# A recurrent attention kernel: one home for the x rows, the residual rows in the place of the attention weights, and an eighth of a streamed weight unit kept in SBUF

## The chip, the cores and the metric

The kernel runs on one core of a Trainium2 chip. The metric is the device time of one execution in microseconds (us); the figure for a kernel is the median of several runs. A profile is one execution recorded instruction by instruction. In it, PE is TensorE (matmuls), PEld its weight loads, DVE is VectorE, ACT is ScalarE, POOL is GpSimd and SP is SyncE, which here only issues DMAs.

## The reference

The output is the sum of three things over 2048 tokens of width 1024: the input, a dense part, and a recurrent attention part. Both parts work on the layer-normed input `xn`.

```python
def _A_ref(x, mem0, Wq, Wk, Wv, Wo, seg_len):      # seg_len 32, 32 heads of 128
    scale = Dh ** (-0.5)                           # M = 8 memory rows
    mask = (idx[:, None] < M) | (idx[:, None] >= idx[None, :])
    mem = mem0
    for s in range(n_seg):                         # 64 segments
        h = concatenate([mem, xs], axis=1)         # 8 + 32 rows
        q, k, v = h @ Wq, h @ Wk, h @ Wv
        p = softmax(where(mask, q @ k.T * scale, -1e9))
        o = (p @ v) @ Wo
        mem = o[:, :M, :]                          # the next segment's memory
        outs.append(o[:, M:, :])
    return concatenate(outs, axis=1)

def _B_ref(x, w1, b1, w2, b2):                     # 1024 -> 3584 -> 1024
    return gelu(x @ w1 + b1) @ w2 + b2

return x + _A_ref(xn, ...) + _B_ref(xn, ...)
```

A segment's memory is the attention output of the segment before it, so the 64 segments run one after the other.

## The kernel before

**Two phases.** The first phase computes the layer norm, the dense part and the input's own share of the sum, and writes the sum of these two to DRAM as *residual rows* (`res_d`, and `resL_d` for the left rows below). It also writes the normed input, transposed, as *x rows* (`rows_d`). In the second phase the 64 segments run in order. The index of a segment within a group of four is called `i4`.

**Left rows.** A segment has 32 x rows and 8 memory rows, 40 in all, while TensorE's column tiles here are 32 wide. So each segment's main pass carries 24 of the x rows and the 8 memory rows. The last 8 x rows of four segments are *left rows*, 32 together, and go through the same weights in passes of their own, spread over the segments of a group. Their output product runs in segments with `left_o` (`i4 == 1`, and the last one): 16 times, and once more at the end.

**The weights.** The four projections are 64 *units* of 128 x 2048 bf16 numbers (512 KB): the half passes K0, Q0, K1, Q1, V0 and V1 of eight units each, and O with sixteen. 47 units stay in SBUF. 17 do not fit and are *streamed*: 15 of them come from DRAM in every segment, and two are kept in four PSUM banks and copied by VectorE (`copy_bits`, line 273). There are six slots for streamed units. When a unit has been used (`unit_done`), SP issues the DMA of the next streamed unit into its slot (`start_stream`, line 284). So the order of the transfers is the order of the units, six ahead at most.

**One segment.** The x rows with the memory rows are TensorE's weights in the K, Q and V passes (line 830); they stand in one of two homes of 128 x 256, `homes[s % 2]`, the two halves of `hr_home`. While the passes run, scores, exponentials, sums and the weighted values of the two halves of heads are put between units at fixed positions (`SCORES_0`, `SUMS_0`, `VALUES_1` and so on). `sums` writes the attention weights to `pd_main` (line 1012), and `values` reads them (lines 1039 and 1045). The output pass O (`o_product`, line 1088) has 16 positions. In segments without left rows a position before the ninth takes two blocks of 256 columns per matmul, and later ones take one block; in segments with left rows all take two. Then `put_mem` turns the 8 memory rows and VectorE copies them into the next segment's x rows (line 330). The next K0 waits for this copy. After it, VectorE adds the residual rows (line 1246), and the sums are stored.

**Small DMAs of a segment.** They are issued by ACT in the first seven segments and by POOL after (`loads`). Ahead of the V passes the x rows of the next segment are loaded into the idle home (line 1155). After V1 the segment's own home is free, and the residual rows are loaded into it (line 1185); the sum is made in place, and four stores write it to the output from there (line 1279). In segments with left rows, the left residual rows are loaded to `pd_main` after position 6 of O (line 1211), the left sum is also made in place, and each of the two sums goes to a DRAM scratch `outL_d` in two stores of 64 partitions (line 1252). From there POOL copies the rows to the output, at the `unit_done` of the following segment (line 1276).

**Who shares which memory.** `v_home`, `outM` and the queries' home `q_home` are one stretch of the tile `kq`: `v_home` (512 columns) holds V and then, as `outM`, the second half of heads' values and the memory rows' source; `q_home` (640 columns) begins at the same column, and the next segment's queries are written to it (lines 909 and 925). `nat_home` is the first 512 columns of `d_oL`; it holds the first half of heads' values, which positions 0 to 7 of O read, and then the next segment's keys (line 882).

The order on each engine is the order in which the program is written (a manual schedule); waits between engines, and between a DMA and who reads or rewrites its memory, are put in by the framework as semaphores.

Of the kernel before, what the change touches and what calls it, by code (L numbers as in the profile page):

```python
# [10 lines left out]
BF16 = mybir.dt.bfloat16  # L11
# [3 lines left out]
ALU = mybir.AluOpType  # L15
PSUM = bass.MemoryType.PSUM

P = 128
S = 2048
DM = 1024  # L20
# [4 lines left out]
SEG = 32  # L25
MEM = 8
NSEG = S // SEG
KT = DM // P
# [9 lines left out]
NX = 24  # L38
NL = SEG - NX
GRP = 4  # L40
NGRP = NSEG // GRP
# [71 lines left out]
STREAMED_O = [unit for unit in ORDER[48:] if IS_STREAMED[unit]]  # L113

IN_BANKS = STREAMED_O[AT_BANKS]
KEPT = (IN_PSUM, IN_BANKS)
assert len(RESIDENT) == NUNIT - STREAMED


@with_exitstack  # L120
def kernel(
# [16 lines left out]
    nc = tc.nc  # L138
# [3 lines left out]
    out_flat = out.rearrange("b s d -> (b s) d")  # L142
# [6 lines left out]
    Wo_v = A_Wo.rearrange("h e d -> e h d")  # L149
# [8 lines left out]
    rowsL_d = dram.tile([NGRP + 1, P, 256], BF16, name="rowsL_d")  # L158
    resL_d = dram.tile([NGRP + 1, P, 256], BF16, name="resL_d")
    R_n = dram.tile([S, DM], BF16, name="R_n")  # L160
    outL_d = dram.tile([NGRP, 2 * SEG, DM], BF16, name="outL_d")


    place = nc.lookup_mloc("DynamicDMAScratchLoc")
# [15 lines left out]
    hrp = ctx.enter_context(tc.tile_pool(name="hrp", bufs=1))  # L180
    ctx.enter_context(tc.manual_schedule())

    homes = [hr_home[:, 0:256], hr_home[:, 256:512]]
    small_consts = consts.tile([P, 16], BF16, name="small_consts")
    bd, off = small_consts[:, 0:4], small_consts[:, 4:8].bitcast(F32)

# [3 lines left out]
        return slabs.tile([P, 2048], BF16, name="u", tag=place)  # L190


    ident = homes[1][:, 0:P]
    make_identity(nc, ident)
    ident_mem = nc.alloc_sbuf_tensor_at("ident_mem", [P, 4, NL], BF16, offset=SCRATCH + 3712)[:, :, :]
    nc.vector.tensor_copy(out=ident_mem[:, :, :], in_=ident.rearrange("p (j t) -> p j t", j=4)[:, :, NX:SEG])
# [78 lines left out]
    def start_stream(slot):  # L275
        if not starts:
            return
        n = starts.popleft()
        unit, t = streams[n], slab(slot)
        if unit in kept_in:  # L280
            for c0, bank in kept_in[unit]:
                copy_bits(t[:, c0:c0 + 1024].bitcast(U32), bank.bitcast(U32))
        elif unit in copies:
            nc.sync.dma_start(out=t[:, :], in_=copies[unit])
        else:
            fetch(t[:, :], unit)
        stream_tiles[n], slot_of[n] = t, slot
# [1 line left out]
    nxt, kept_in = {}, {}  # L289

    def load_x_rows(s, eng=nc.sync):
        eng.dma_start(out=homes[s % 2], in_=rows_d[s, :, :])
        nxt["hT"] = homes[s % 2].rearrange("p (k t) -> p k t", k=KT)

    def load_left_rows(g, eng=nc.sync):
        hr = hrp.tile([P, 256], BF16, name="hrL")
        eng.dma_start(out=hr[:, :], in_=rowsL_d[g, :, :])
        nxt["hL"] = hr.rearrange("p (k t) -> p k t", k=KT)
# [50 lines left out]
    with tc.tile_pool(name="ma", bufs=2) as ma:  # L349
# [235 lines left out]
        for tg in range(4):  # L585
            last = tg == 3
            if last:

                load_x_rows(0)
                load_left_rows(0)  # L590
                h = 4 * IN_BANKS[1] + 2 * IN_BANKS[2]
                nc.sync.dma_start(out=kq[:, 0:DM], in_=Wo_v[:, h, :])
                start_stream("xn0")
                start_stream("xn1")
                fetch_resident("late2", "xt0", "xt1")
# [140 lines left out]
    with tc.tile_pool(name="late", bufs=1) as late:  # L736
# [66 lines left out]
        for s in range(NSEG):  # L803
# [257 lines left out]
            def o_columns(t, k, blocks):  # L1061

                c0 = DM * k + 256 * blocks[0]
                if len(blocks) == 1:
                    return t[:, c0:c0 + 256]
                d = blocks[1] - blocks[0]
                return t[:, c0:c0 + 256 * (d + 1)].rearrange("p (n c) -> p n c", c=256)[:, ::d, :]

            def o_product(n, t, acc):


                unit = O_UNITS[n]
                w, i, u = unit
                for k in range(2):
                    h = 4 * (i % 4) + 2 * u + k
                    main = (outM if i >= 4 else nat_home)[:, h, :]
                    if left_o:
                        lhs = [(0, 32, left_outs[i // 4][:, h, :]), (32, 32, main)]
                        tiles = [(64 * r + r0, w, (2 * r, 2 * r + 1), lhsT) for r0, w, lhsT in lhs for r in range(2)]
                        start, stop = n == 0 and k == 0, n == 15 and k == 1  # L1080
                    elif n < NPAIR:
                        tiles = [(64 * k + 32 * r, 32, (r, r + 2), main) for r in range(2)]
                        start, stop = n == 0, n == NPAIR - 1
                    else:
                        tiles = [(32 * r, 32, (r,), main) for r in range(4)]
                        start, stop = n == NPAIR and k == 0, n == 15 and k == 1
                    for r0, rows, blocks, lhsT in tiles:
                        nc.tensor.matmul(  # L1088
                            acc[r0:r0 + rows, 0:256 * len(blocks)],
                            lhsT=lhsT,  # L1090
                            skip_group_check=True,
                            rhs=o_columns(t, k, blocks),
                            start=start,
                            stop=stop,
                            tile_position=(0, r0),
                        )
# [54 lines left out]
            turn_q(psQ1, (0, 10, 16))  # L1151
            if left_q[1] and not first:
                turn_qL(psQ1L, 1)
            if not final:
                load_x_rows(s + 1, loads)
            psV, psVL = half_pass("V", 0, left_v[0], {})
            if left_v[0]:
                left_values(0, psVL)
# [26 lines left out]
            loads.dma_start(out=homes[s % 2], in_=res_d[s + 1, :, :])  # L1185
            if first:
                load_left_rows(g + 1, loads)

# [8 lines left out]
            if apart:  # L1197
                at[VALUES_1[i4] + 1] = [moved_values]
            psX = new_acc()
            for n, unit in enumerate(O_UNITS):  # L1200
                t = unit_tile(unit)
                if n == NPAIR and not left_o:
                    st["folded"] = fold(psX)
                    psX = new_acc()
                o_product(n, t, psX)
                unit_done(unit)
                for fn in at.get(n, ()):
                    fn()
                if n == 6 and left_o:
                    st["resL"] = pd_main[:, 0:256]  # L1210
                    loads.dma_start(
                        out=st["resL"], in_=resL_d[og, :, :]
                    )
            nw = 2 if left_o else 1
            if not final:
                o_sb = outM
# [20 lines left out]
            res, rows = homes[s % 2], slice(s * SEG, s * SEG + NX)  # L1237
            tiles = (res, st["resL"]) if left_o else (res,)
            for w, r in reversed(list(enumerate(tiles))):
                if left_o:  # L1240
                    o = psX[:, 256 * w:256 * w + 256].rearrange("p (h e) -> p h e", e=32)
                else:
                    o = o_sb[:, 0:8, :]
                r_rows = r.rearrange("p (h e) -> p h e", e=32)
                to = d_oL[:, 256 * w:256 * w + 256].rearrange("p (h e) -> p h e", e=32) if final else r_rows
                nc.vector.tensor_tensor(out=to, in0=o, in1=r_rows, op=ALU.add)  # L1246
                if left_o and not final:

                    for b in range(2):
                        c0 = 256 * (2 * b + w)  # L1250
                        eng = nc.scalar if w else nc.gpsimd
                        eng.dma_start(out=outL_d[og, :, c0:c0 + 256], in_=r[64 * b:64 * b + 64, :])
# [5 lines left out]
            if final:  # L1258
                engines = [nc.sync, nc.scalar]
                n = 0  # L1260
                for b in range(2):
                    cs = slice(512 * b, 512 * b + 512)
                    pieces = [(rows, slice(64 * b + m0, 64 * b + m0 + NX))]
                    for sl, row in left_rows:
                        p0 = 64 * b + NL * sl
                        pieces.append((slice(row, row + NL), slice(p0, p0 + NL)))
                    for o, i in pieces:
                        engines[n % 2].dma_start(out=out_flat[o, cs], in_=d_oL[i, 0:512])
                        n += 1
            elif left_o:  # L1270
                pairs = [(out_flat[rows, :], outL_d[og, m0:m0 + NX, :])]
                pairs += [
                    (out_flat[row:row + NL, :], outL_d[og, NL * sl:NL * sl + NL, :]) for sl, row in left_rows
                ]
# [42 lines left out]
```

## Time and profile before

| | us |
|---|---|
| median of 3 runs | 1795.1 (1793.92 to 1796.6) |
| profiled execution, whole time | 1796.11 |
| its span, first to last instruction | 1794.4 |
| PE busy | 1696.3 (95%) |
| PEld busy | 889.3 (50%) |
| DVE busy | 983.8 (55%) |
| ACT busy | 683.6 (38%) |
| POOL busy | 300.4 (17%) |
| DMA moved | 594.44 MB, mean 331 GB/s |
| of it by SP's queue | 567.08 MB, 84.4% of the time of 16 DMA engines |
| granted TensorE clock | 1.000 |

The segments take the time from about 405 us on, some 21.5 us each. Of a row of the profile such as "L1012 DVE TENSOR_TENSOR pd_main<-kq,mixed 128x320 ... x128 | 62.5, 488 | 130.2 <-ACT mixed L999 130.2", L1012 is the line of the kernel, then come the engine, the operation, what is written from what, the shape, how often, the busy time in all, the mean of one in ns, and the idle time of the engine just before with what ended it. A row of waits reads: who waited, for whom, us in total, how often, the longest. A row of a timeline reads: start, duration, engine, line, operation, and in brackets the idle time before it and what ended it. ACTq and SPq are an engine's sequencer, which issues DMAs.

### The profile page before, as it was taken

How to read it: one execution, taken by the hardware profiler on the slowest of the kernel's cores; microseconds unless marked ns; L12 is line 12 of the kernel's file. 1: busy time of each engine (PE TensorE's matmuls, PEld its weight loads, DVE VectorE, ACT ScalarE, POOL GpSimd, SP SyncE). 2: the span in 40 equal slices, each digit the busy share in tenths (PEclk: the TensorE clock that was granted, in tenths of full speed). 3: DMA queues.
4: the chain of work that ended last, by engine and by line, in shares of the span. 5: the costliest groups of instructions: out<-in, count | busy, mean ns of one | idle time of the engine just before them, and what ended most of it. 6: DMA issues, size and time to landing. Idle time of an engine off the chain costs nothing.

```text
span 1794.4 us, 71508 instructions
## 1 busy us (share of the span) xinstructions
PE 1696.3 (95%) x31164; PEld 889.3 (50%) x31164; DVE 983.8 (55%) x2514; ACT 683.6 (38%) x1692; POOL 300.4 (17%) x586
## 2 busy tenths in 40 slices
PE   9999999999999999999999999999999989999988
PEld 5444444444555555545454555554545544554544
DVE  7656483825555555555455555555555554555544
ACT  6344251603333333334343434343434333433333
POOL 0000002301231111212122121121121111111111
PEclk9999999999999999999999999999999999999999
DMA  9455312789999999999999999999999999999998
GB/s 279 144 169 165 87 48 73 267 277 371 391 385 383 387 376 384 377 379 382 365 394 371 390 386 398 378 393 372 374 382 384 385 371 369 380 383 381 370 386 316
DMA packets 232830, 594.44 MB, mean 331 GB/s; under 512 B 57715, under 2 KB 88035, under 8 KB 232516
## 3 DMA queue, kind: packets, MB, share of 16 engines
q1 hardware_dynamic: 197584, 567.08, 84.4%
q0 software_dynamic: 16896, 16.85, 2.9%
q10 hardware_dynamic: 18036, 5.94, 1.3%
q8 instruction: 244, 4.00, 0.9%
q14 instruction: 70, 0.57, 0.1%
HBM read 573.43 MB, written 28.90 MB: 336 GB/s over the span
## 4 chain that ended last, share of the span: by engine, by line
PE 75%; DMA 11%; ACT 4%; DVE 4%; issue 4%; ACTq 1%; SPq 1%; POOL 0%; DVEq 0%; POOLq 0%
PE acc L830 38%; PE acc L1088 12%; PE ps L534 10%; DMA u<-Wc_O 8%; PE ps L662 6%; PE ps L693 3%; DMA u<-Wc_V 2%; ACT mixed L999 2%; PE acc L1039 1%; PE mixed L947 1%; DVE kq L914 1%; ACTq L459 1%; DVE pd_main L1012 1%; ACT kq L909 1%; SPq L521 1%
## 5 line engine op out<-in xcount | busy, mean ns | idle before, releaser
L830 PE MATMUL acc<-u,hr_home 128*32 128x512 bf16 x11520 | 758.8, 380 | 14.7 <-issue 8.3
L830 PEld LDWEIGHTS <-hr_home 128*32 128x32 bf16 x12288 | 350.3, 96 | 281.1 <-issue 33.2
L830 PE MATMUL acc<-u,hrL 128*32 128x512 bf16 x2880 | 256.2, 380 | 2.6 <-DVE qL L882 1.0
L534 PE MATMUL ps<-u 128*128 128x512 bf16 (+1 forms) x992 | 195.0, 358 | 0.0
L273 DVE TENSOR_SCALAR u<-kept 128x512 uint32<-128x512 uint32 x254 | 163.2, 684 | 56.9 <-PE acc L830 43.2
L1088 PE MATMUL acc<-u,d_oL 128*32 128x512 bf16 x2592 | 168.9, 380 | 13.1 <-issue 7.9
L882 ACT CAST d_oL<-acc 128x512 bf16<-128x512 f32 x143 | 82.0, 584 | 256.8 <-PE acc L830 251.5
L1088 PE MATMUL acc<-u,kq 128*32 128x256 bf16 (+1 forms) x2884 | 135.8, 310 | 13.6 <-DMA u<-Wc_O 11.2
L662 PE MATMUL ps<-u 128*128 128x512 bf16 x672 | 146.0, 379 | 0.0
L534 PEld LDWEIGHTS <-u 128*128 128x128 bf16 x992 | 91.6, 98 | 101.5
L1088 PEld LDWEIGHTS <-kq 128*32 128x32 bf16 x3908 | 103.0, 96 | 75.4 <-ACT kq L1058 21.2
L1012 DVE TENSOR_TENSOR pd_main<-kq,mixed 128x320 bf16<-128x320 bf16 x128 | 62.5, 488 | 130.2 <-ACT mixed L999 130.2
L914 DVE STREAM_TRANSPOSE kq<-kq 128x512 bf16<-128x512 bf16 x128 | 91.0, 711 | 73.2 <-ACT kq L909 71.0
L909 ACT CAST kq<-acc 128x512 bf16<-128x512 f32 (+2 forms) x192 | 85.4, 445 | 112.2 <-PE acc L830 82.6
L1279 POOL DMA_DIRECT2D out_dram<-hr_home x168 | 85.4, 516 | 221.7 <-DVE hr_home L1246 221.7
L886 ACT CAST kq<-acc 128x512 bf16<-128x512 f32 x128 | 75.2, 588 | 112.2 <-PE mixed L953 112.2
L830 PEld LDWEIGHTS <-hrL 128*32 128x32 bf16 x3072 | 87.9, 96 | 58.5 <-issue 7.6
L977 DVE TENSOR_TENSOR kq<-kq,mixed 128x96 bf16<-128x96 bf16 (+1 forms) x256 | 38.1, 190 | 125.8 <-ACT kq L967 72.6
L662 PEld LDWEIGHTS <-u 128*128 128x128 bf16 x672 | 65.5, 98 | 78.8 <-DVE u L619 0.4
L611 ACT ACTIVATE u<-ps,b1col 128x512 bf16<-128x512 f32 x112 | 76.5, 684 | 65.4 <-PE ps L534 62.3
L1088 PEld LDWEIGHTS <-d_oL 128*32 128x32 bf16 x2592 | 64.6, 96 | 67.7 <-issue 20.8
L999 ACT ACTIVATE mixed<-mixed,small_consts 128x160 f32<-128x160 f32 x256 | 94.2, 368 | 8.4
(126 smaller groups left out, 1911.2 us busy)
## 6 DMA issues: line engine op xcount, KB each, us to landing
u<-Wc_K SPq DMA_DIRECT2D x256, 512.0 KB
u<-Wc_V SPq DMA_DIRECT2D x256, 512.0 KB
u<-Wc_O SPq DMA_DIRECT2D x256, 512.0 KB
u<-Wc_Q SPq DMA_DIRECT2D x192, 512.0 KB
u<-in_B_w_dram SPq DMA_DIRECT2D x28, 512.0 KB
u<-in_A_Wq_dram SPq DMA_DIRECT2D x13, 512.0 KB
u<-in_A_Wv_dram SPq DMA_DIRECT2D x12, 512.0 KB
u<-in_A_Wk_dram SPq DMA_DIRECT2D x9, 512.0 KB
```

What stands on the lines that cost most here:

```text
L273: nc.vector.tensor_single_scalar(out=out, in_=in_, scalar=0, op=ALU.bitwise_or)
L534: nc.tensor.matmul(ps[:, SEG * s0:SEG * s1].rearrange("p (s t) -> p s t", t=SEG), lhsT=w1_sb[fb // 2][:, kt, (fb % 2) * P:(fb % 2 + 1) * P ...
L611: nc.scalar.activation(out=xb[:, :], in_=ps[:, :], func=ACT.Identity, bias=b1col[:, fb:fb + 1], scale=1.0)
L662: nc.tensor.matmul(ps[:, :], lhsT=gts[fc // 4][:, fc % 4, t * P:(t + 1) * P], rhs=w2_sb[fc // 2][:, fc % 2, cs], start=(fc == 0), stop=(fc ...
L830: nc.tensor.matmul(o, lhsT=lhs[:, i, :], rhs=m, start=(i == seq[0]), stop=(i == seq[-1]), tile_position=(0, 32 * j),)
L882: cp(out=out, in_=ps.rearrange("p (h e) -> p h e", e=32))
L909: nc.scalar.copy(out=q_home[:, h0:h1, NL:40], in_=ps[:, 32 * h0:32 * h1].rearrange("p (h e) -> p h e", e=32))
L914: nc.vector.transpose(out=home, in_=home)
L999: nc.scalar.activation(out=mixed[:, 160 * b:160 * b + 160], in_=mixed[:, 0:160], func=ACT.Exp, scale=-1.0, bias=off[:, b:b + 1],)
L1012: nc.vector.tensor_tensor(out=pdA.rearrange("p c b q -> p b c q"), in0=prA[:, None, :, :].to_broadcast([P, 2, 4, 40]), in1=dd, op=ALU.mult,)
L1088: nc.tensor.matmul(acc[r0:r0 + rows, 0:256 * len(blocks)], lhsT=lhsT, skip_group_check=True, rhs=o_columns(t, k, blocks), start=start, sto ...
L1279: loads.dma_start(out=out_flat[rows, 256 * j:256 * j + 256], in_=res[32 * j:32 * j + NX, :])
```

## The change

- `hr_home` now holds one home for the x rows; its other half, `part`, holds 256 of the 2048 columns of one streamed unit, `IN_PART` (the fourth streamed unit of O, at position 13). `part` is loaded once, in the dense phase. The unit's DMA in each segment is 1792 columns wide instead of 2048.
- Where a matmul of that unit took two blocks at once of which the last is kept, it is split into two of 256 columns each. That concerns segments with left rows: 68 more matmuls and weight loads in all.
- The x rows of the next segment are loaded after V1, into the one home, by ACT in all segments.
- The residual rows are loaded to `pd_main` after position 6 of O, the left residual rows to the first half of `nat_home` (`d_oL`) after position 8, both by ACT. The main sum is made in `pd_main` and stored from there. The left sum is made in `v_home` and stored from there.
- Each of the two sums of a segment with left rows goes to `outL_d` in one store of 128 partitions instead of two of 64; the layout of `outL_d` follows, and the copies from it to the output have two pieces per row.

```diff
-    homes = [hr_home[:, 0:256], hr_home[:, 256:512]]
+    home, part = hr_home[:, 0:256], hr_home[:, 256:512]
...
         elif unit in copies:
-            nc.sync.dma_start(out=t[:, :], in_=copies[unit])
+            c1 = 2048 - (256 if unit == IN_PART else 0)
+            nc.sync.dma_start(out=t[:, 0:c1], in_=copies[unit][:, 0:c1])
...
     def load_x_rows(s, eng=nc.sync):
-        eng.dma_start(out=homes[s % 2], in_=rows_d[s, :, :])
-        nxt["hT"] = homes[s % 2].rearrange("p (k t) -> p k t", k=KT)
+        eng.dma_start(out=home, in_=rows_d[s, :, :])
+        nxt["hT"] = home.rearrange("p (k t) -> p k t", k=KT)
...
+                w, i, u = IN_PART
+                nc.sync.dma_start(out=part, in_=Wo_v[:, 4 * i + 2 * u + 1, 768:1024])
...
+                if unit == IN_PART and k == 1 and blocks == (3,):
+                    return part
...
-                    for r0, rows, blocks, lhsT in tiles:
+                    if unit == IN_PART and k == 1:
+                        apart = [(r0, rows, (b,), lhsT, at) for at in range(len(tiles[0][2])) for r0, rows, blocks, lhsT in tiles for b in blocks[at:at + 1]]
+                    else:
+                        apart = [(*tile, 0) for tile in tiles]
+                    for r0, rows, blocks, lhsT, at in apart:
...
-            if not final:
-                load_x_rows(s + 1, loads)
             psV, psVL = half_pass("V", 0, left_v[0], {})
...
-            loads.dma_start(out=homes[s % 2], in_=res_d[s + 1, :, :])
+            if not final:
+                load_x_rows(s + 1, nc.scalar)
...
+            res, resL = pd_main[:, 0:256], d_oL[:, 0:256]
...
-                if n == 6 and left_o:
-                    st["resL"] = pd_main[:, 0:256]
-                    loads.dma_start(
-                        out=st["resL"], in_=resL_d[og, :, :]
-                    )
+                if n == 6:
+                    nc.scalar.dma_start(out=res, in_=res_d[s + 1, :, :])
+                if n == 8 and left_o:
+                    nc.scalar.dma_start(out=resL, in_=resL_d[og, :, :])
...
-                nc.vector.tensor_tensor(out=to, in0=o, in1=r_rows, op=ALU.add)
+                at = 256 * w
+                sums_at = d_oL[:, at:at + 256] if final else v_home[:, 0:256] if w else res
+                nc.vector.tensor_tensor(
+                    out=sums_at.rearrange("p (h e) -> p h e", e=32), in0=o, in1=r_rows, op=ALU.add
+                )
                 if left_o and not final:
-
-                    for b in range(2):
-                        c0 = 256 * (2 * b + w)
-                        eng = nc.scalar if w else nc.gpsimd
-                        eng.dma_start(out=outL_d[og, :, c0:c0 + 256], in_=r[64 * b:64 * b + 64, :])
+                    eng = nc.scalar if w else nc.gpsimd
+                    eng.dma_start(out=outL_d[og, :, 256 * w:256 * w + 256], in_=sums_at)
```

More of the change, by code (lines that the diff above doesn't have):

```diff
@@ L116 @@
 KEPT = (IN_PSUM, IN_BANKS)
+IN_PART = STREAMED_O[3]
 assert len(RESIDENT) == NUNIT - STREAMED
@@ L160 @@
     R_n = dram.tile([S, DM], BF16, name="R_n")
-    outL_d = dram.tile([NGRP, 2 * SEG, DM], BF16, name="outL_d")
+    outL_d = dram.tile([NGRP, P, 512], BF16, name="outL_d")
     place = nc.lookup_mloc("DynamicDMAScratchLoc")
@@ L190, in slab @@
         return slabs.tile([P, 2048], BF16, name="u", tag=place)
-    ident = homes[1][:, 0:P]
+    ident = part[:, 0:P]
     make_identity(nc, ident)
@@ L1059, in values, with o_columns @@
                     let_go(av[r])
-            def o_columns(t, k, blocks):
+            def o_columns(unit, t, k, blocks):
+                if unit == IN_PART and k == 1 and blocks == (3,):
+                    return part
                 c0 = DM * k + 256 * blocks[0]
@@ L1086, in o_product @@
                         start, stop = n == NPAIR and k == 0, n == 15 and k == 1
-                    for r0, rows, blocks, lhsT in tiles:
+                    if unit == IN_PART and k == 1:
[3 more added lines that the diff above has]
+                    for r0, rows, blocks, lhsT, at in apart:
                         nc.tensor.matmul(
-                            acc[r0:r0 + rows, 0:256 * len(blocks)],
+                            acc[r0:r0 + rows, 256 * at:256 * (at + len(blocks))],
                             lhsT=lhsT,
                             skip_group_check=True,
-                            rhs=o_columns(t, k, blocks),
+                            rhs=o_columns(unit, t, k, blocks),
                             start=start,
@@ L1236 @@
                     lead_products(LEAD)
-            res, rows = homes[s % 2], slice(s * SEG, s * SEG + NX)
-            tiles = (res, st["resL"]) if left_o else (res,)
+            rows = slice(s * SEG, s * SEG + NX)
+            tiles = (res, resL) if left_o else (res,)
             for w, r in reversed(list(enumerate(tiles))):
@@ L1244 @@
                 r_rows = r.rearrange("p (h e) -> p h e", e=32)
-                to = d_oL[:, 256 * w:256 * w + 256].rearrange("p (h e) -> p h e", e=32) if final else r_rows
-                nc.vector.tensor_tensor(out=to, in0=o, in1=r_rows, op=ALU.add)
+                at = 256 * w
[3 more added lines that the diff above has]
+                )
                 if left_o and not final:
-                    for b in range(2):
-                        c0 = 256 * (2 * b + w)
-                        eng = nc.scalar if w else nc.gpsimd
-                        eng.dma_start(out=outL_d[og, :, c0:c0 + 256], in_=r[64 * b:64 * b + 64, :])
+                    eng = nc.scalar if w else nc.gpsimd
+                    eng.dma_start(out=outL_d[og, :, 256 * w:256 * w + 256], in_=sums_at)
             let_go(psX)
@@ L1270 @@
             elif left_o:
[L1271 to L1274, printed above, removed]
+                made = outL_d[og, :, :].rearrange("(b r) c -> r b c", b=2)
+                pairs = [(out_flat[rows, :], made[m0:m0 + NX, :, :])]
+                pairs += [(out_flat[row:row + NL, :], made[NL * sl:NL * sl + NL, :, :]) for sl, row in left_rows]
+                pairs = [(o.rearrange("r (b c) -> r b c", b=2), r) for o, r in pairs]
                 for o, r in pairs:
```

## The prediction

> **What bounds the kernel now.** I read the page's slices first, then stretches of the span, then the waits, then the timeline at the places that the change touches.
>
> The page, time in 40 slices:
>
> ```profile
> PE   9999999999999999999999999999999989999988
> ...
> DMA  9455312789999999999999999999999999999998
> GB/s 279 144 169 165 87 48 73 267 277 371 391 385 383 387 376 384 377 379 382 365 394 371 390 386 398 378 393 372 374 382 384 385 371 369 380 383 381 370 386 316
> ```
>
> From slice 10 on (the 64 segments) both TensorE and the DMA engines are full. The stretches say how near to its limit each is. Segments 8 and 11 alone, then segments 8 to 59 together (us, busy time of the five engines, clock, DMA share, GB/s):
>
> ```profile
> 585.60:606.55 20.95, 20.21 (x470) 11.26 (x462) 11.77 (x32) 8.35 (x23) 3.74 (x7) 1.00 1.02 392
> ...
> 650.14:671.97 21.83, 20.34 (x470) 11.31 (x462) 11.26 (x30) 9.04 (x24) 3.78 (x7) 1.00 1.02 389
> 585.60:1705.90 1120.30, 1050.63 (x23694) 571.41 (x23686) 599.02 (x1549) 428.54 (x1170) 206.83 (x390) 1.00 1.00 380
> ```
>
> 1120.3 us for 52 segments is 86.2 us for a cycle of four (i4 = 0 to 3). The transfers could run at about 390 GB/s and run at 380: alone they would need 86.2 x 380/390 = 84.0. For TensorE I added up, from the starts of its streaming matmuls (lines 830 and 1088, normally 0.22 us per four), all that exceeds this spacing: 45.6 us in the 52 segments, 3.5 per cycle, nearly all at units that come from DRAM. So TensorE's own path is 86.2 - 3.5 = 82.7. The transfers bind by a little, and lateness of TensorE is partly free: 3.5 us per cycle is waiting for DMA anyway.
>
> The waits name those places, and a second kind, at the scores:
>
> ```profile
> PE acc L1088 <- DMA u<-Wc_O: 16.1, 27, 1.6
> PE mixed L947 <- DVE kq L914: 12.9, 40, 0.5
> ...
> PE acc L830 <- DMA u<-Wc_V: 5.4, 10, 1.3
> ```
>
> How long a small DMA takes beside this traffic stands at the lines of the residual load, the left residual load, the out stores, in this order (all POOL's, min/median/max), and in the chain:
>
> ```profile
> DMA to landing us min/median/max: 3.3/5.6/6.4
> ...
> DMA to landing us min/median/max: 2.9/4.7/5.5
> ...
> DMA to landing us min/median/max: 4.1/4.9/6.9
> ...
> 450.65 6.61 DMA pd_main<-resL_d
> ```
>
> The last was issued by ACT. ACT's other loads of the first seven segments show no landing, but VectorE waits for two: the residual issued at 493.19 released it at 499.63 (6.4 us), a left residual issued at 537.54 at 543.67 (6.1).
>
> **The change part by part**, in us after the last V1 matmul of a segment, the "own path" being segments without a DMA wait.
>
> *Bytes.* 64 KB of 15 streamed 512 KB units per segment stay in SBUF: 0.8% of 84.0 per cycle, -0.67. Against it, two loads per segment (x rows, residual) go from POOL to ACT. In the packet records POOL's 64 KB are 16 packets of 4096 bytes at 174 ns, ACT's 128 packets of 512 at 27.5 ns: 2.78 against 3.52 us of one engine, 0.046 of sixteen, twice per segment +0.37 per cycle. Transfers after: 83.7 (bounds 83.3, if small packets slip between large ones, to 84.0).
>
> *x rows.* Before, they were loaded into the idle one of two homes ahead of the V passes. Now the one home is V1's operand, so the load starts after V1 and is needed at the put of the memory rows (the copy on line 330), which waits for it, and the next segment's first matmul for that. The place in ACT's order is that of the old residual load, which ACT issued at 0.98 (i4 = 0 and 1), 0.67 (2) and 1.36 (3, where a second cast goes before it):
>
> ```profile
> 493.11 0.59 ACT L882 CAST kq<-acc 128x512 bf16<-128x512 f32 x1 [0.44 <-DVE kq L1017]
> 493.19 0.36 ACTq L1185 DMA_DIRECT2D hr_home<-res_d  x1
> ...
> 498.05 0.23 DVE L330 CAST hr_home<-mixed 128x64 bf16<-128x64 f32 x1 [0.57 <-PE mixed L320]
> ...
> 499.63 0.29 DVE L1246 TENSOR_TENSOR hr_home<-kq,hr_home 128x256 bf16<-128x256 bf16 x1 [1.36 <-DMA hr_home<-res_d]
> ```
>
> A load from here landed 1.4 us after the memory rows' copy; that was only VectorE's sum, now it is the copy itself. On the own path the copy starts at 5.8, 8.55, 6.2, 5.85 (i4 = 0 to 3). ACT's loads took 6.1 to 6.7, POOL's 4.7 when fewer streamed transfers were outstanding. TensorE will be later and fewer will be outstanding, so I take 5.5, between them: ready at 6.5, 6.5, 6.2, 6.9, late by 0.7, 0, 0, 1.05, in sum +1.7 per cycle. By 4.7: +0.2; by 6.7: 1.9 + 0 + 1.2 + 2.2 = +5.3.
>
> *Residual and out stores.* The residual (ACT, position 6 of O, issued near 2.4) lands at 7.9; VectorE's sum ends near 8.4 instead of 6.3 to 7.8. Next in VectorE's queue are the copies of the kept unit (1.3 us) and, 2.3 us after the copy of line 330, a transpose: covered. The four POOL stores now read pd_main and land 6.8 us after the sum (before: sum ended 6.7, last landed 13.4 for i4 = 0), at 15.2. The next weights are written to pd_main 9.0 to 9.2 after the copy of line 330, at 15.5 or later. Margin 0.3 to 0.8: I take 0; without it, up to 0.3 in three segments, +1.
>
> *Left sums (after i4 = 1).* The left residual goes to d_oL, which position 7 of O still reads: issue at 4.0, landed at 9.5 where the sum could start at 8.7. The sum goes to v_home, and ACT stores it from there 0.4 after the sum's start, at 9.9 (before, from pd_main, on average 9.8). The store lands 4.9 later, at 14.8. But v_home is where the next segment's queries are written: VectorE's left queries and ACT's cast both have to wait for this store, while before nothing wrote pd_main for 8.7 us. Segment 10's start shows when they come:
>
> ```profile
> 630.45 1.12 ACTq L1252 DMA_DIRECT2D outL_d<-pd_main  x2
> ...
> 633.41 0.18 DVE L925 COPY kq<-mixed 128x128 bf16<-128x128 bf16 x1
> 633.93 0.59 ACT L909 CAST kq<-acc 128x512 bf16<-128x512 f32 x1 [1.20 <-PE acc L830]
> 634.55 0.71 DVE L914 STREAM_TRANSPOSE kq<-kq 128x512 bf16<-128x512 bf16 x1 [0.96 <-ACT kq L909]
> 635.32 0.20 PE L947 MATMUL mixed<-kq,d_oL 128*32 128x40 bf16 x4
> ```
>
> Cast, transpose and scores follow without slack, 3.5 us after the store's issue. The own path has the cast at 12.6; 14.8 makes the scores, and all of TensorE behind them, 2.2 later. Bounds: loads of 4.7 and the quickest store (4.1) give +0.6, 6.7 and 5.8 give +4.3.
>
> *The rest.* 68 more matmuls of 256 columns take the place of halves of 512: the row has 273 against 380 ns, four side by side, 0.1 per cycle (0 to 0.2). ACT's issues cost 0.33 each, in gaps of 1 us and more: 0; without gaps 0.33 x 9. One store per left sum instead of two spares 0.5 of issue on ACT and POOL, already in the 4.9. The kept block costs one 64 KB load in the dense phase, 0.2.
>
> **Sum.** Own path 82.7 + 1.7 + 2.2 + 0.1 = 86.7; transfers 83.7. Now TensorE binds, by 3.0. Before, the cycle was 2.2 above the longer of the two, which stood 1.3 apart; at 3.0 apart I take 0.6 of DMA waits (0 to 2.2). Cycle 87.3, +1.1, times 63/4: +17 us. The profiled execution (1796.1, span 1794.4) is 1.0 above the median, 1795.1, so the prediction is 1812. 0.2% (3.6 us) is about what measuring this kernel can tell from no change.
>
> In the Trainium skill, "DMA: Bandwidth & Descriptors", section "Anatomy of one DMA — SWDGE (gpsimd) path", fits a DMA by 2.0 us + bytes/436e3: an estimate of 2.15 us for 64 KB. By it, no store or load here would be late and the sum would be the first rival's. The trace's 5.6 and 4.9 speak against it, in this traffic.
>
> **The rivals.** *1, faster: nothing lands late.* The left residuals landed in 4.7, the last ones, with hardly a stream outstanding, in 2.9. If TensorE's first lateness thins the queue so far that x rows land within 4.5 us of issue (5.85 - 1.36), and left residual plus store within 8.2 (12.6 - 4.0 - 0.4), both waits vanish, and the transfers bind: 83.7 + 2.2 = 85.9, or 85.5 at their lower bound: -5 to -11, 1784 to 1790. Against it: no POOL store landed within 4.1, and the outstanding amount at these places was 2 to 3 units. 15%.
>
> *2, slower by much: latencies stay as ACT's were.* At 6.1 the x rows cost 1.3 + 0.5 + 1.6 = 3.4, the left store 4.0 + 6.1 + 0.4 + 4.9 - 12.6 = 2.8: own path 89.0, 0.4 of waits, +3.2: 1845. For it: all ACT loads that VectorE waited for. Against: these were in the first segments, where other copies ran too. 15%.
>
> *3, no change: the lateness is covered.* It falls where DMA waits follow in the same cycle; if the 3.5 and the 0.3 of bytes cover all of 4.0, the cycle stays at 86.2: 1795. Against: the remaining waits must go to nothing. 10%.
>
> *4, the byte saving does not show,* because the packets of 512 bytes cost it all: transfers 84.0, which the sum with TensorE binding hardly feels; inside the range of mine.
>
> **How the numbers follow.** My sum 60%, its own range 1800 to 1832. Slower 0.75 (mine and rival 2), within 0.2% 0.10 (rival 3), faster 0.15 (rival 1). From 1789 to 1845 holds eight in ten.
>
> **What would show it.** The copy of the memory rows (line 330 before) released by the x-row load, about 1 us late in i4 = 3 segments and not at all after i4 = 1; the casts of queries after each left segment released by the outL store, the scores 2 us later; Wc_O waits below 16.1; DMA share and GB/s below 380. Wrong if the landings of ACT's small DMAs are 4.5 or less, or if out stores hold up pd_main.

## The result

The changed kernel takes 1849.4 us (median of 6 runs, 1842.67 to 1868.28) where the kernel before takes 1794.5: the ratio is 1.0318, 95% interval 1.0267 to 1.0369. The forecast was 1812, 1789 to 1845. The direction was right and the loss three times the size.

The page of the changed kernel, time in 40 slices, and the shares of the chain that ended last:

```profile
PE   9999999999898989999888998899989999989887
...
DMA  9464314879999999999999999999999999999998
GB/s 273 140 189 138 101 31 117 285 275 369 375 370 361 364 347 369 362 369 372 362 336 368 376 380 351 362 369 373 372 355 368 374 361 376 379 362 370 353 373 302
...
PE 50%; DMA 30%; DVE 7%; ACT 5%; issue 4%; POOL 1%; ACTq 1%; SPq 1%; DVEq 0%; POOLq 0%
PE acc L834 22%; PE ps L536 10%; DMA hr_home<-rows_d 9%; PE ps L666 6%; DMA pd_main<-res_d 5%; PE acc L1098 5%; DMA out_dram<-pd_main 5%; DMA outL_d<-kq 4%; PE ps L697 3%; DMA u<-Wc_V 2%; DMA d_oL<-resL_d 2%; DVE kq L918 2%; ACT mixed L1003 2%; DVE pd_main L1016 2%; DMA u<-Wc_O 1%
```

The dense phase is as before. In the segments less is moved per second, and the chain runs through small DMAs: x rows, residual, out stores, left store. The streamed units, which had 8% (Wc_O) and 2% (Wc_V) of the chain before, now have 1% and 2%.

Segments 8 to 59 as one stretch (us, busy time of PE, PEld, DVE, ACT, POOL, clock, DMA share, GB/s):

```profile
592.40:1750.50 1158.10, 1058.10 (x23738) 570.30 (x23738) 599.61 (x1547) 428.20 (x1170) 139.06 (x260) 0.99 0.99 365
```

1158.1 us for 13 cycles of four segments is 89.1 per cycle, against 86.2: +2.9, times 63/4 = 46 us. That is all that the profiled executions differ by (1842.7 - 1796.1); the changed kernel's profiled run is the fastest of its six, and the median adds some 8 us more. This stretch is 38 us longer than before; TensorE's busy time in it rose by 7 (1058 against 1051; a part of this is matmuls at half the clock, see the last section), and the rest went into waits. What TensorE waits for:

```profile
PE mixed L951 <- DVE kq L918: 40.1, 66, 2.4
PE acc L834 <- DVE hr_home L332: 34.6, 40, 2.2
...
PE acc L834 <- DMA u<-Wc_V: 4.1, 6, 1.3
PE acc L1098 <- DMA u<-Wc_O: 3.6, 8, 0.7
```

The first (scores behind the queries' transpose) was 12.9, the second (K0 behind the memory rows) was 0.9, and the two waits for units were 5.4 and 16.1. What stands behind the first two, in the list of all waits:

```profile
DVE hr_home L332 <- DMA hr_home<-rows_d: 63.0, 44, 2.8
...
ACT kq L913 <- DMA outL_d<-kq: 41.4, 16, 3.6
...
DVE kq L929 <- DMA outL_d<-kq: 26.9, 16, 2.8
...
DVE pd_main L1016 <- DMA out_dram<-pd_main: 18.0, 13, 2.0
```

Each is a memory that now has two uses within a few microseconds: the one x home, v_home under the left store, pd_main under the out stores. The first in an i4 = 3 segment, in the timeline:

```profile
1124.42 0.58 ACT L886 CAST kq<-acc 128x512 bf16<-128x512 f32 x1 [0.42 <-DVE kq L1021]
1124.50 0.33 ACTq L294 DMA_DIRECT2D hr_home<-rows_d  x1
...
1130.20 0.23 DVE L332 CAST hr_home<-mixed 128x64 bf16<-128x64 f32 x1 [1.58 <-DMA hr_home<-rows_d]
1130.48 0.62 PE L834 MATMUL acc<-low,hr_home 128*32 128x512 bf16 x8 [0.98 <-DVE hr_home L332]
```

V1 ended at 1123.15. ACT's sequencer issues the load 1.35 later, behind the second cast; its landing releases the copy 5.7 after that, and the copy and K0 stand still for it. The second, after a segment with left rows:

```profile
1176.29 0.33 ACTq L1261 DMA_DIRECT2D outL_d<-kq  x1
...
1180.79 0.23 DVE L929 COPY kq<-mixed 128x128 bf16<-128x128 bf16 x1 [1.47 <-DMA outL_d<-kq]
1180.84 0.58 ACT L913 CAST kq<-acc 128x512 bf16<-128x512 f32 x1 [2.27 <-DMA outL_d<-kq]
1181.46 0.71 DVE L918 STREAM_TRANSPOSE kq<-kq 128x512 bf16<-128x512 bf16 x1 [0.45 <-ACT kq L913]
1182.22 0.20 PE L951 MATMUL mixed<-kq,d_oL 128*32 128x40 bf16 x4 [1.05 <-DVE kq L918]
```

The store takes 4.5 us. VectorE's left queries and ACT's cast are released by the same landing, and cast, transpose and scores follow as a chain.

### The profile page after: what moved, and what is told of

Its sections match the earlier page's. It is cut to its first block, busy times and chain, and to the rows that moved or that the text cites. A ratio compares the mean times of both kernels' runs of the same rounds, so it can differ in the third digit from the quotient of the medians.

```text
span 1841.0 us, 71649 instructions
## 1 busy us (share of the span) xinstructions
PE 1703.2 (93%) x31212; PEld 888.7 (48%) x31232; DVE 984.2 (53%) x2514; ACT 683.1 (37%) x1692; POOL 225.1 (12%) x442
## 4 chain that ended last, share of the span: by engine, by line
PE 50%; DMA 30%; DVE 7%; ACT 5%; issue 4%; POOL 1%; ACTq 1%; SPq 1%; DVEq 0%; POOLq 0%
PE acc L834 22%; PE ps L536 10%; DMA hr_home<-rows_d 9%; PE ps L666 6%; DMA pd_main<-res_d 5%; PE acc L1098 5%; DMA out_dram<-pd_main 5%; DMA outL_d<-kq 4%; PE ps L697 3%; DMA u<-Wc_V 2%; DMA d_oL<-resL_d 2%; DVE kq L918 2%; ACT mixed L1003 2%; DVE pd_main L1016 2%; DMA u<-Wc_O 1%
## 5 line engine op out<-in xcount | busy, mean ns | idle before, releaser
L834 PEld LDWEIGHTS <-hr_home 128*32 128x32 bf16 x12288 | 346.2, 97 | 323.9 <-DVE hr_home L332 60.4
L1288 POOL DMA_DIRECT2D out_dram<-pd_main x168 | 85.9, 515 | 433.5 <-DVE pd_main L1256 430.1
L1098 PE MATMUL acc<-u,kq 128*32 128x512 bf16 (+1 forms) x2871 | 132.1, 308 | 6.5 <-DMA u<-Wc_O 2.8
L834 PEld LDWEIGHTS <-hrL 128*32 128x32 bf16 x3072 | 85.3, 97 | 63.3 <-issue 12.9
L834 PE MATMUL acc<-low,hr_home 128*32 128x512 bf16 x768 | 62.4, 387 | 34.8 <-DVE hr_home L332 34.6
```

The lines of the kernel that those rows point to most:

```text
L834: nc.tensor.matmul(o, lhsT=lhs[:, i, :], rhs=m, start=(i == seq[0]), stop=(i == seq[-1]), tile_position=(0, 32 * j),)
L1098: nc.tensor.matmul(acc[r0:r0 + rows, 256 * at:256 * (at + len(blocks))], lhsT=lhsT, skip_group_check=True, rhs=o_columns(unit, t, k, block ...
```

## The experiments

Theory A: these three waits are the loss. Theory B: the loss lies in ACT's queue and its small packets, or is covered, so that taking a wait away shows little. Ratios are to the kernel before, on the same chip, with 95% intervals; "cycle" is the length of four segments (8 to 59) in the profiled execution, where the kernel before has 86.2 and the changed one 89.1. Differences between kernels are taken from ratios, 0.001 being 1.8 us.

**The changed kernel without the kept block.**

```diff
-            c1 = 2048 - (256 if unit == IN_PART else 0)
+            c1 = 2048
...
-                if unit == IN_PART and k == 1 and blocks == (3,):
-                    return part
```

> The changed kernel without the kept block: the unit is streamed whole and its matmuls are not split; all else as changed. Theory A (three reuses of memory hold TensorE up: the single home by 2.5 us per cycle of four segments, v_home under the left store by 1.6, pd_main under the out stores by 1.2; TensorE's own path binds): the 64 KB per segment are nearly hidden, 0 to 6 us slower than the changed kernel. Theory B (the transfers still bind and the waits are covered by them; the loss comes from the loads' small packets on ACT's queue): 8 to 11 us slower (0.67 us per cycle).

1862.9 us, ratio 1.0359 (1.0324 to 1.0393), cycle 89.5. That is 7 us above the changed kernel, with intervals that overlap, and between the two forecasts, which it does not separate. The block does not cost anything, and what it gives is small. This kernel is the base of the next two, since it leaves half of hr_home free.

**The left sum in the free half.**

```diff
-                sums_at = ... else v_home[:, 0:256] if w else res
+                sums_at = ... else part if w else res
```

> As the one without the block, and the left sum is written to the free half of hr_home and stored from there, so that no later write waits for this store. Theory A: 1.6 us less per cycle, so 20 to 30 us faster than the one without the block, and the scores of i4 = 2 segments 5.4 us after the memory rows' copy again instead of 7.0. Theory B: 0 to 8 us faster.

1835.1 us, ratio 1.021 (1.0186 to 1.0235), cycle 88.6: 27 us less than its base by the ratios, 14 (0.9 per cycle) by the profiled cycles. The scores come 5.6 us after the memory rows' copy again (6.9 in its base), and the waits for outL_d on the queries are gone from the list. Theory A.

**Two homes for the x rows, loaded ahead of V0.**

```diff
-        eng.dma_start(out=home, in_=rows_d[s, :, :])
+        eng.dma_start(out=(home, part)[s % 2], in_=rows_d[s, :, :])
...
+            if not final:
+                load_x_rows(s + 1, nc.scalar)
             psV, psVL = half_pass("V", 0, left_v[0], {})
...
-            if not final:
-                load_x_rows(s + 1, nc.scalar)
```

> As the one without the block, and the x rows go to two homes in turn, loaded by ACT ahead of the V passes; residual, left sum and stores as changed. Theory A: 2.5 to 2.9 us less per cycle, so 35 to 45 us faster than the one without the block; no copy of the memory rows waits for a DMA. Theory B: 0 to 10 us faster.

1825.2 us, ratio 1.0154 (1.0127 to 1.0181), cycle 87.7: 37 us less than the base, as theory A expected, but 1.9 per cycle where it had 2.5 to 2.9. In none of segments 8 to 59 does the memory rows' copy wait for a DMA. ACT still issues these loads: where they have time in hand, its issue does no harm.

**The changed kernel with the x rows loaded by POOL.**

```diff
-                load_x_rows(s + 1, nc.scalar)
+                load_x_rows(s + 1, loads)
```

> The changed kernel, kept block and single home included, but the x rows are loaded by POOL from the eighth segment on. POOL has nothing ahead of the load, so it issues about 0.3 us after V1 instead of 0.64 to 1.15, and its loads took 5.6 us to landing where ACT's now take about 6.1. Theory A: x rows ready near 5.9 us after V1 against 6.85 to 7.0, the copy of the memory rows waits 0.1 to 0.3 us instead of 0.8 to 1.0 in three segments of four: 25 to 35 us faster than the changed kernel. Theory B: only the packets change (0.046 us per segment): 0 to 5 us faster.

1829.0 us, ratio 1.0158 (1.011 to 1.0207), cycle 87.9: 29 us below the changed kernel by the ratios, 19 (1.2 per cycle) by the profiled cycles. Waits of this kernel, and the landing of the load, both to be held against 63.0 in 44 waits:

```profile
DVE hr_home L332 <- DMA hr_home<-rows_d: 22.5, 22, 2.0
```

```profile
DMA to landing us min/median/max: 4.1/5.6/6.9
```

Nothing is changed in the program but the engine that issues, and with it the packets. POOL issues 0.2 to 0.5 us after V1 instead of 0.64 to 1.15, and the copy starts at 6.3, 6.45 and 5.8 us (i4 = 0, 2, 3) instead of 6.8, 7.0 and 6.85. So the loss follows the time at which x rows land, as A says; ACT's later issue and longer landing are a part of that lateness.

**One part of the change alone: late x rows in the kernel before.**

```diff
-            if not final:
-                load_x_rows(s + 1, loads)
             psV, psVL = half_pass("V", 0, left_v[0], {})
...
+            if not final:
+                load_x_rows(s + 1, nc.scalar)
             loads.dma_start(out=homes[s % 2], in_=res_d[s + 1, :, :])
```

> The kernel before with one part of the change alone: the x rows, still in two homes, are loaded by ACT after V1 instead of ahead of V0. Theory A (the copy of the memory rows waits for them in three segments of four, 2.5 to 3 us per cycle, and some of it is made up at later waits for DMA): 25 to 45 us slower than the kernel before. Theory B (in the kernel before the waits for DMA cover it): under 10 us slower.

1838.7 us, ratio 1.0255 (1.022 to 1.029), cycle 88.4: +46 us (25 to 45 were expected), from one load moved behind V1. Its waits of TensorE:

```profile
PE acc L830 <- DVE hr_home L330: 50.5, 44, 2.6
PE mixed L947 <- DVE kq L914: 14.0, 43, 0.5
PE acc L1088 <- DMA u<-Wc_O: 11.2, 26, 0.9
```

From the spacing of matmul starts, K0 stands 3.6 us per cycle at the memory rows. The cycle grew by 2.3: the waits for streamed units gave back the rest, 0.9 of it within the streamed passes (3.5 to 2.6, and 0.2 of the 2.6 is matmuls at half the clock, see the last section). So late x rows are covered to about a third. Here the load shares its time with the residual's, and the copy starts at 7.4 to 7.6, later than in the changed kernel.

**Both: two homes, and the left sum in the spent home.**

```diff
-                sums_at = ... else v_home[:, 0:256] if w else res
+                sums_at = ... else (home, part)[s % 2] if w else res
```

> The changed kernel without the block, with two homes for the x rows, and with the left sum written to the home that V1 has just done with: two of the three reuses are gone, pd_main under the out stores is left. Theory A, waits that add: 38 + 28 us below the one without the block, less what pd_main (1.2 us per cycle, 19 us) has taken over: 1797 to 1815. Rival (each wait hides another, so two removals give little more than the larger): about 1825.

1811.8 us, ratio 1.0093 (1.0058 to 1.0128), cycle 86.5. From the two homes alone it is 11 us less, with intervals that just touch (1.1 per cycle, 18 us, in the profiles), within what theory A left room for. What remains is the wait of the weights for the out stores:

```profile
DVE pd_main L1014 <- DMA out_dram<-pd_main: 25.9, 17, 2.6
```

**And the main sum in the spent home.**

```diff
-                sums_at = ... else (home, part)[s % 2] if w else res
+                sums_at = ... else (home, part)[s % 2] if w or not left_o else res
...
-                    loads.dma_start(out=out_flat[rows, 256 * j ... in_=res[32 * j ...
+                    loads.dma_start(out=out_flat[rows, 256 * j ... in_=sums_at[32 * j ...
```

> As the one before, and in segments without left rows the main sum is written to the spent home and stored from there, so that the next attention weights wait for no store. Only ACT in POOL's place, the residual in pd_main and the single left stores remain of the change. Theory A: level with the kernel before, 0 to 6 us above it (0.37 us per cycle for ACT's small packets); no wait of the weights for the out stores. Rival (ACT's queue itself is the loss): 10 us or more above the kernel before.

1806.0 us, ratio 1.0066 (1.0034 to 1.0097), cycle 86.1. That wait is gone, and the cycle is that of the kernel before. The step itself is 0.4 per cycle, 5 us by ratios with overlapping intervals. In the steady segments of the profiled execution, then, nothing is left of the loss, though ACT issues all the loads; as an account of the cycle, theory B falls. For the whole kernel theory A's forecast (0 to 6 us above the kernel before) missed: 0.66% is 12 us, on the rival's side (10 or more). The two profiled executions differ by 6 of them: 2 in the dense phase, 2 in segments 0 to 7 and 3.5 after segment 59, less 1 in the cycles. The 2 in the dense phase say little, since the next run, whose dense phase is that of the kernel before, is 2 us longer there too. What makes the rest is open, and ACT's issues at the two ends are not ruled out.

**The bytes of the block alone, in the kernel before.**

```diff
-            nc.sync.dma_start(out=t[:, :], in_=copies[unit])
+            c1 = 2048 - (256 if unit == STREAMED_O[3] else 0)
+            nc.sync.dma_start(out=t[:, 0:c1], in_=copies[unit][:, 0:c1])
...
+                if unit == STREAMED_O[3] and k == 1 and blocks[-1] == 3:
+                    blocks = tuple(b - 1 for b in blocks)
```

> The kernel before, in which the DMA of that one unit is 1792 columns wide and the last 256 columns are not loaded; the matmuls of these columns read the 256 columns ahead of them, so a piece of Wo is left out of the result and its neighbour counted twice. Nothing is moved. It prices the block alone: 0.67 us per cycle if the transfers bind, 8 to 11 us faster than the kernel before. Rival (TensorE's waits for DMA come from the order of the units, not from the bytes): 0 to 3 us faster.

1793.1 us, ratio 0.9992 (0.9969 to 1.0015), cycle 85.9. The expectation missed: 8 to 11 us lie outside the interval (up to 5.6 us). The cycle is 0.24 shorter, not 0.67.

**Half of the streamed O units.**

```diff
+            c1 = 1024 if unit in STREAMED_O else 2048
...
+                if unit in STREAMED_O[:AT_BANKS]:
+                    k = 0
```

> The kernel before, in which the four streamed units of O are loaded 1024 columns wide, and the matmuls of their second halves read the first halves: half of these four units is left out of the result. 1 MB of 7.9 per segment falls away, nothing else changes. Theory T (the transfers bound the kernel before, and all of TensorE's 3.5 us per cycle of waits in the streamed passes were theirs): the cycle falls to TensorE's own 82.7, 50 to 58 us faster. Theory O (the waits come from when units are due, not from the sum of bytes): 10 to 30 us faster.

1768.1 us, ratio 0.9856 (0.9806 to 0.9905), cycle 83.8: 26 us for 13% of the streamed bytes, theory O. The stretches of the kernel with the block's bytes alone (the run before this) and of this one, over the same segments, in this order:

```profile
587.80:1704.90 1117.10, 1050.11 (x23690) 573.33 (x23689) 598.94 (x1547) 428.73 (x1170) 206.83 (x390) 1.00 1.00 379
```

```profile
586.00:1676.10 1090.10, 1043.40 (x23691) 565.39 (x23694) 598.53 (x1548) 428.32 (x1170) 206.04 (x390) 1.00 0.95 341
```

In the second the transfers run at 341 GB/s, far below the 379 of the first, and TensorE's streamed passes still have 2.2 us of waits per cycle out of 3.5 in the kernel before. The waits for units of O (16.1 us in the kernel before) are gone from the list, and those for units of V have grown from 5.4:

```profile
PE acc L831 <- DMA u<-Wc_V: 9.2, 19, 1.4
```

So fewer bytes helped at the units that they shortened, and a sum of bytes over one ceiling does not describe the rest. That the rest hangs on when a unit's slot comes free and how long its transfer takes is likely, but no run here takes it apart. 1 MB per segment bought 2.3 us per cycle; at that rate the block's 64 KB buy 0.14.

**The left sum over the kept block, loaded again once per cycle.**

```diff
-                sums_at = ... else v_home[:, 0:256] if w else res
+                sums_at = ... else part if w else res
...
+            if i4 == 2:
+                loads.dma_start(out=part, in_=Wo_v[:, 4 * IN_PART[1] + 2 * IN_PART[2] + 1, 768:1024])
```

> The changed kernel, block and single home kept, but the left sum is written over the kept block, stored from there, and the block loaded again (64 KB) in the segment after, once per cycle. Theory A: the left store's wait (1.6 us per cycle) goes, a fourth of the block's saving goes too: 18 to 28 us faster than the changed kernel. Rival (the wait of left stores is covered by the x rows' in this kernel): under 8 us.

1838.9 us, ratio 1.0269 (1.0227 to 1.0311), cycle 88.2: 9 us below the changed kernel, with intervals that overlap, 15 us (0.9 per cycle) by the profiled cycles. By the ratio that lies between the two forecasts. The scores are at their old distance (5.7 us after the copy), so the wait went, but about half of its 1.6 us came back as a new one: TensorE waits for the reload of the block, 0.8 us per cycle.

```profile
PE acc L1098 <- DMA hr_home<-in_A_Wo_dram: 11.3, 9, 2.0
```

The reload takes 5.3 to 5.9 us to landing, and position 13 of O in the same segment reads it.

**Three cures at once,** on top of the last: x rows by POOL, and

```diff
-                    loads.dma_start(out=out_flat[rows, 256 * j ...
+                    (loads, nc.scalar)[j % 2].dma_start(out=out_flat[rows, 256 * j ...
```

> The changed kernel with three cures together: x rows loaded by POOL (20 us in a run of its own), left sum over the kept block with one reload per cycle (10 us), and the four out stores issued by ACT and POOL in turn, so that the last is issued 1 us earlier (pd_main, 6 to 18 us). If the three waits are the loss and add: 1800 to 1812. It passes the kernel before (1795) only if the kept block itself gains, which the bytes alone, within 0.3% of no change, did not show.

1819.4 us, ratio 1.0147 (1.0121 to 1.0172), cycle 87.5, above the 1800 to 1812 that were expected. The wait for pd_main is nearly gone (1.6 us, once), and two others have come:

```profile
ACT d_oL L886 <- DMA out_dram<-pd_main: 70.1, 12, 9.0
ACT d_oL L886 <- DVE pd_main L1258: 37.5, 10, 6.3
```

ACT's stores wait for VectorE's sum, which waits for the late residual, and the next keys' cast (line 886) stands behind them in ACT's order. The two rows count ACT's idle time, not the delay: after segments with i4 = 0 and 3 the cast starts on average 0.9 and 0.7 us after the end of the K0 that it reads, where it was 0.05 in the changed kernel. TensorE's wait for the reloaded block is here too (12.2 us in 9 waits). Also, in i4 = 2 segments POOL issued the x rows 1.8 us after V1.

**The same with POOL's stores, and ACT's load of x rows in i4 = 2.**

```diff
-                load_x_rows(s + 1, nc.scalar)
+                load_x_rows(s + 1, nc.scalar if i4 == 2 else loads)
```

> As the three cures together, but all four out stores are POOL's again (in the run before, ACT's keys' cast stood behind ACT's two stores, which wait for the late residual), and in i4 = 2 segments, where POOL has the copies of the left rows ahead of it and issued the x rows 1.8 us after V1, ACT loads them. If those two were what the cures cost: x rows and left sum by themselves, 20 + 10 us below the changed kernel and up to 10 more, 1805 to 1820, with the wait of the weights for the out stores back. If late loads of whatever kind remain the loss: as the run before, 1819. In no case under the kernel before.

1818.0 us, ratio 1.0159 (1.0118 to 1.02), cycle 87.0. No different from the run before; the time lies in the first forecast and next to the second, and does not separate them. The x rows still hold the copy up (23.6 us in 22 waits), the weights wait for the stores again (13.2 in 11), and TensorE for the reloaded block (6.3 in 7). No cure here keeps the single home and gets under the kernel before, and with the block worth 2 to 4 us by the two runs on bytes (7 by the run without it, inside the noise) there is little to get.

## Why the prediction was wrong, by its steps

*What binds: wrong.* "The transfers bind by a little", with a ceiling of 390 GB/s, gave the block 0.67 us per cycle. The run with its bytes alone showed 0.24 and no change that can be measured, and 13% fewer bytes took 1.3 of TensorE's 3.5 us of waits away, not all. The full DMA rows of the profile were taken for a ceiling.

*DMA waits as cover: the step that failed most.* The sum let them fall from 3.5 to 0.6 per cycle. In the changed kernel the same count in the streamed passes is 3.0; of it 1.2 is released by ACT or VectorE, and 0.45 (5.8 us in 13 cycles) is no wait but matmuls at half the clock (last section), which leaves 1.3 at most for DMA. Measured likewise, the kernel before had 3.1, and no half clock. Lateness was covered by 1.8, not by 2.9. Late x rows alone say the same: 3.6 of wait, 2.3 of loss.

*x rows: place and mechanism right, size too small.* From issue to the copy's start it is 6.2, 6.4 and 5.7 us (i4 = 0, 2, 3; two of 13 in the last class did not wait), where 5.5 was taken between POOL's and ACT's rows. The copy starts at 6.84, 7.03 and 6.85, 2.9 us per cycle above the own path instead of 1.75; i4 = 1 does not wait, as forecast. ACT's 6.1, dismissed as belonging to the first segments, was the right row. "Fewer outstanding, so quicker" did not hold for it. The Trainium skill's fit of a DMA ("DMA: Bandwidth & Descriptors", "Anatomy of one DMA — SWDGE (gpsimd) path"), 2.0 us plus bytes/436e3 or 2.15 us for 64 KB as an estimate, would have had no x row late. Here POOL's loads of x rows took 4.1 to 6.9, and the measurement decides.

*The left store: right.* Issue 9.95 (forecast 9.9), the cast released at 14.5 (14.8), the scores 1.85 late against the own path (2.2); 0.3 of this stood already in the copy (8.85 against 8.55).

*pd_main: given as 0, measured 1.2.* The sum ended at 8.6 and 8.85 in i4 = 0 and 2 (forecast 8.4) and the stores landed at 15.8 and 16.0 (15.2), so the next weights are 9.35, 9.9 and 9.25 us after the copy instead of 9.2, 9.15 and 9.0. The bound of +1 that was worked out for it was the better value, and out stores holding up pd_main was one of the prediction's own signs of being wrong. Taken away as the last of the three waits, it was worth 0.4 us per cycle.

*The sum.* 86.7 of own path and 0.6 of waits were forecast; 89.1 less 1.3 of waits and 0.45 of half clock is 87.3 of own path. Of the 1.8 us per cycle that were missed, 0.7 is the cover, 0.6 own path, and 0.45 the half clock behind long waits, which the sum did not have. The terms cannot simply be added, as the sum did: measured each by its own lateness they are 2.9, 1.85 and 1.2, with the 0.1 for the added matmuls 6.0, while the own path grew by 4.6 from 82.7. The cycles make 28 of the 37 us that were missed; most of the rest is that the median lies 6.7 above the profiled execution, where the prediction took it 1.0 below. Rival 2, latencies as ACT's were, at 1845, was nearest; it had 15%, and its split of the cycle (89.0 of own path, 0.4 of waits) was not what came.

## What to carry to other kernels

A buffer that gets a second use moves its load to the point where the first use ends; count the load's whole landing time, taken from the engine that will issue it and in the traffic it will meet, from there to its first reader. A store's source is taken until the store lands: look up who writes that memory next, however harmless the place looks. And do not count an engine's waits for DMA as cover for lateness, nor a full DMA row as a ceiling, before a run with fewer bytes has shown that bytes bind. Behind a long wait of TensorE look at the granted clock: the wait can cost more than its length.

## What the hardware showed that was not expected

A full DMA row says little of how much is moved. The share was 0.99 at 365 GB/s in the changed kernel and 0.95 at 341 with half of the O units, against 1.00 at 380 before. In the packet records the same 4096-byte packet took 170 ns on average at 380 GB/s, 174 at 365 and 180 at 341: packets last longer when fewer bytes move. Why was not tried.

Some long waits were followed by half the clock. In segments 8 to 59 of the changed kernel's profiled execution there are four stretches of 3.4 us in which the granted clock is 0.50; a matmul of 512 columns takes 0.63 us in them instead of 0.38. The kernel before has none in these segments, nor has the one with all three waits taken away. All four come within 1.1 us of the end of a wait of K0 for the memory rows' copy of 1.8 to 2.2 us, in segments where that copy had waited for x rows. One of them, first the wait in the timeline, then the stretch, with the clock as the third number from its end:

```profile
1106.78 0.62 PE L834 MATMUL acc<-low,hr_home 128*32 128x512 bf16 x8 [1.80 <-DVE hr_home L332]
1107.32:1110.73 3.41, 3.41 (x40) 1.38 (x36) 1.29 (x2) 0.00 (x0) 2.07 (x4) 0.50 0.91 313
```

By the spacing of the matmuls they cost 5.8 us, 0.45 per cycle: it looks like a second price of the late x rows. Three other idle stretches of TensorE, of 1.75, 2.0 and 2.4 us, had none behind them, so length alone does not settle it. In the six runs of the changed kernel the mean granted clock goes from 0.997 down to 0.992, and the slowest run, 1868.3 us, has the lowest; whether this makes the rest of the median's 8 us was not tried.
